# A fused attention and two-layer MoE kernel: routing of the second layer with a tightened span, three rounds for three more experts, and rows turned later

## The chip, the cores and the metric

The kernel runs on one core of a Trainium2 chip. The metric is the device time of one execution in microseconds (us); lower is better. The traces are taken by the hardware profiler on one execution.

## What is computed

The reference chains three parts. Attention: 4 batches, 8 heads, 768 positions, head size 64, a causal window of 128 and 4 sink positions. A first mixture of experts (MoE): each of the 3072 tokens (512 features) goes to the expert with its largest logit. A second MoE, the part that the change touches: every expert takes exactly 384 tokens, given out greedily over the sorted logits.

```python
def _moe2_ref(x, w_gate, w1, w2):
    N, D, E, F = (3072, 512, 8, 1024)
    cap = N // E
    logits = x @ w_gate
    order = np.argsort(-logits.flatten())
    for idx in order:                 # largest logit first
        tok, e = (int(idx) // E, int(idx) % E)
        if assigned[tok] >= 0 or counts[e] >= cap:
            continue
        assigned[tok] = e
        counts[e] += 1
    for e in range(E):
        h = np.maximum(x[assigned == e] @ w1[e], 0.0)
        out[assigned == e] = h @ w2[e]
```

## The kernel before, in words

The change is in the second MoE, which starts at about 519 us. Two things run interleaved there, in one program order that the Python code writes out.

**The expert FFN** (`Ffn.run`, from L823). The experts are worked off one after the other, 384 tokens each, in 8 chunks s of 128 hidden features. A chunk is 12 matmuls into ph (L1036: four parts d of the 512 features, three products each of a high and a low part, in place of one float32 product), then ScalarE's relu hh (L1046) and VectorE's remainder hl (L1047), and 9 matmuls into y0 to y2 (L950, helper mm3) for an earlier chunk. Weights are split into high and low parts ahead of use: w1h, w2h on ScalarE (L917, L897), w1l on VectorE or POOL (L922), w2l on POOL (L901).

Between groups of matmuls of a chunk, `side(q)` (L995) is called for q = 0 to 3: after half of the ph matmuls, after all of them, after the first y group, at the end. It splits a weight, turns rows, and calls `tick` (L942), which calls the router's `pop`, asks for weights (`poll_w`) and for the next gather (`poll_x`, L874). `src.pop()` offers the router three more places in a chunk.

**Turning rows.** An expert's rows come by three indirect DMAs (parts a) into xg, issued by POOL (`xget`, L1890). They must be transposed: `xprep` (L789) does it for one of four feature parts d: three transposes on TensorE into the PSUM bank tr (L796), ScalarE's high part xh (L797), VectorE's low part xl (L798). There is one bank tr, so a turning waits until both have read the one before. The tuple xp says at which (chunk of the expert, q) the next expert's parts are turned: (6,0), (6,2), (7,0), (7,2).

**The router** (`Route.steps`, L1914) finds for the next expert in order the logit bound above which exactly 384 free tokens lie. One round `it` compares all best logits with 64 bounds (`compare`, L1675, on VectorE), counts by 13 small matmuls (L1693, helper `count`), compares the counts with 384 (gs, gg), spreads the result by one matmul (L1976), takes maxima (J8), and sets the next, 62 times finer bounds (b0, b1, lop, lo). POOL keeps a 1x1 copy of b0 (L1957). Experts 0 to 2 in this order have three rounds each (L1940: `last`), experts 3 to 6 have four; the eighth takes what is left. After the rounds the chosen tokens A are taken out of L, and the span for the next expert's first round is set from the last bound and lb[k+1], a lower bound that the preparation before had found (L2012 to L2016).

**Compaction** (`compact`, L1899, `compact_steps`, L1482) turns A into a list of 384 row numbers idx: a prefix matmul (L1498), one-hot compares on VectorE, 26 matmuls (L1523). Then the gather may be issued.

**The order.** `Route.pop` (L1829) is offered a place some seven times per chunk, and issues a step of the compaction and one of the rounds, each only if the planner's TensorE clock has come to the time the step asked for, and if its VectorE clock is at most half a microsecond ahead of TensorE's (SLACK). These clocks are the planner's estimates; they set only the order of the program. `force_x` (L1874) issues compaction steps without asking when rows are to be turned and no list is there.

The end of expert k's second layer is copied out by `yout` (L2051) and scattered by indirect DMAs on POOL (L2055).

Of the kernel before, what the change touches and what calls it, by code (L numbers as in the profile page):

```python
# [779 lines left out]
class Ffn:  # L780
# [42 lines left out]
    def run(self, js, w1, w2, src, yout, hook=None, xp=((6, 0), (6, 2), (7, 0), (7, 2)), LEAD=3, LAG=2, pre=None, onx=None, more=(), mark=lambda s, n: None):  # L823
# [108 lines left out]
        def prep(j, d, tag="tr"):  # L932
            if j not in xgs:
                src.force_x(j)
                clk.pe = max(clk.pe, clk.dve)
                wantx.remove(j)
                xgs[j] = src.xget(j)
            if d == 0 and onx is not None:
                onx(j, xgs[j])
            self.xprep(j, src.width(j), xgs[j], d, tag)  # L940

        def tick():  # L942
# [3 lines left out]
            poll_x()  # L946
# [44 lines left out]
        for s in range(last + 1):  # L991
# [3 lines left out]
            def side(q):  # L995
# [9 lines left out]
                if jx + 1 < len(js) and s < total:  # L1005
                    for d in range(4):
                        if xp[d] == (f, q):
                            prep(js[jx + 1], d)
                if not ticked:
# [89 lines left out]
class Src:  # L1099
# [15 lines left out]
    wait = 0  # L1115

# [352 lines left out]
SLACK = 0.5  # L1469
SLACK1 = 1.6  # L1470
# [80 lines left out]
class Route(Src):  # L1551
# [4 lines left out]
    def __init__(self, nc, g, pool, xs):  # L1556
# [4 lines left out]
        self.em3 = {}  # L1561
        self.at = [0.0, 0.0]
# [30 lines left out]
         self.half, self.nrow, self.hi, self.J2, self.nv) = (self.sc[:, i:i + 1] for i in range(17))  # L1593
# [59 lines left out]
    def sizes(self, V, pd):  # L1653
# [3 lines left out]
        V.tensor_scalar(self.nrow, self.nbig, 2.0, None, op0=OP.mult)  # L1657

# [170 lines left out]
    def pop(self):  # L1829
        clk = self.g.clk  # L1830
        for i, f in ((1, self.pop_comp), (0, self.pop_main)):
            if clk.pe >= self.at[i] and clk.dve < clk.pe + (SLACK if 1 in self.idx else SLACK1):
# [57 lines left out]
    def xget(self, k):  # L1890
        xg = self.x[k] if k in self.x else self.xp.tile([128, 3, DM], F32, name="xg2", bufs=2)
        for a in range(3):
            self.nc.gpsimd.indirect_dma_start(out=xg[:, a, :], out_offset=None, in_=self.xs,
                                              in_offset=bass.IndirectOffsetOnAxis(ap=self.idx[k][0][:, a:a + 1], axis=0))
        em = self.em3[k] = self.p.tile([1, 1], I32, name="em3", bufs=E)
        self.nc.gpsimd.tensor_copy(em, self.e[k])
        return xg

# [15 lines left out]
    def steps(self):  # L1914
# [16 lines left out]
        for k in range(E):  # L1931
# [4 lines left out]
            if k < E - 1:  # L1936
# [3 lines left out]
                last = NIT - 1 if k == 0 or k > FEW else NIT - 2  # L1940
                for it in range(first, last + 1):
# [11 lines left out]
                    else:  # L1953
                        self.compare(V, slice(0, 2), slice(0, HR), inv)
                        V.tensor_scalar(b0, d, -1.5, lo0 if it == 0 else lo, op0=OP.mult, op1=OP.add)
# [71 lines left out]
            else:  # L2027
# [4 lines left out]
                V.tensor_copy(em, t0[0:1])  # L2032
                nc.tensor.matmul(pc, g.ones, OH, start=True, stop=True, skip_group_check=True)
                nc.scalar.activation(junk, pc, AF.Copy, accum_out=chk[:, 0, k:k + 1])
                self.e[k] = em
                self.comp.append(self.compact(k, A, rs, pre))
# [244 lines left out]
```

## Time and profile before

| | |
|---|---|
| median of 3 runs | 852.79 us (852.39 to 853.32) |
| profiled execution | 853.57 us, span 851.8 us |
| mean granted TensorE clock | 0.992 |
| TensorE busy | 813.5 us, 96% of the span |
| VectorE, ScalarE, POOL busy | 608.7, 384.9, 348.0 us |
| longest chain to the end | PE 78%, DVE 11%, ACT 4% |

In the profile PE is TensorE, PEld its weight load, DVE VectorE, ACT ScalarE, POOL GpSimd, SP the engine that issues most DMAs. A line such as `ph L1036` names the tile and the line of the kernel; all of the router's VectorE instructions have L145, since a helper issues them, and are told apart by their tiles. A duration is that of one instruction as the profiler gives it; matmuls are pipelined, so the time that one holds TensorE's queue is read from its start to the next one's start. In timelines, instructions of one kind in a row are merged (x13), and `[1.13 <-DMA ...]` says how long the engine was idle before and what ended it.

### The profile page before, as it was taken

How to read it: one execution, taken by the hardware profiler on the slowest of the kernel's cores; microseconds unless marked ns; L12 is line 12 of the kernel's file. 1: busy time of each engine (PE TensorE's matmuls, PEld its weight loads, DVE VectorE, ACT ScalarE, POOL GpSimd, SP SyncE). 2: the span in 40 equal slices, each digit the busy share in tenths (PEclk: the TensorE clock that was granted, in tenths of full speed). 3: DMA queues.
4: the chain of work that ended last, by engine and by line, in shares of the span. 5: the costliest groups of instructions: out<-in, count | busy, mean ns of one | idle time of the engine just before them, and what ended most of it. 6: DMA issues, size and time to landing. Idle time of an engine off the chain costs nothing.

```text
span 851.8 us, 15197 instructions
## 1 busy us (share of the span) xinstructions
PE 813.5 (96%) x5001; PEld 651.6 (76%) x5006; DVE 608.7 (71%) x1763; ACT 384.9 (45%) x1091; POOL 348.0 (41%) x574
## 2 busy tenths in 40 slices
PE   8889999998999999999999988999999999999997
PEld 4666666667888888888888746778888888889996
DVE  7888787877579696978878268868688787753320
ACT  6667777764342433344342313334334343434442
POOL 5455967582331101020000004436465656465662
PEclk9999999999999999999999998999999999999999
DMA  7434555666534544444436507334444345345401
GB/s 222 159 107 150 151 144 143 176 217 215 120 84 166 161 136 149 149 148 126 124 104 223 192 14 235 126 110 149 145 155 146 129 151 154 126 161 174 147 39 42
DMA packets 70655, 122.85 MB, mean 144 GB/s; under 512 B 9890, under 2 KB 24102, under 8 KB 70440
## 3 DMA queue, kind: packets, MB, share of 16 engines
q1 hardware_dynamic: 63848, 102.36, 38.0%
q0 software_dynamic: 6720, 19.43, 7.1%
q8 instruction: 42, 0.69, 0.4%
q14 instruction: 45, 0.37, 0.2%
HBM read 102.06 MB, written 19.71 MB: 143 GB/s over the span
## 4 chain that ended last, share of the span: by engine, by line
PE 78%; DVE 11%; ACT 4%; issue 3%; DMA 1%; POOL 1%; DVEq 0%; POOLq 0%; ACTq 0%
PE y L950 29%; PE ph L1036 28%; PE sp L323 4%; PE po L395 3%; ACT P L352 3%; PE tr L796 2%; PE rt L1693 2%; PE pt L360 2%; PE px L431 1%; PE rc L1523 1%; DMA xg<-xs,idx 1%; DVE mx L342 1%; DVE sc L145 1%; PE sp L409 1%; DVE sp L340 1%
## 5 line engine op out<-in xcount | busy, mean ns | idle before, releaser
L1046 ACT ACTIVATE hh<-ph 128x384 fp32r<-128x384 f32 (+1 forms) x112 | 60.2, 538 | 268.2 <-PE ph L1036 267.6
L1036 PE MATMUL ph<-xh,w1h 128*128 128x384 f32 (+1 forms) x448 | 166.9, 372 | 0.8 <-DVE hl L1047 0.8
L1036 PE MATMUL ph<-xh,w1l 128*128 128x384 f32 (+1 forms) x448 | 161.1, 360 | 1.2 <-DVE w1l L922 1.2
L1036 PE MATMUL ph<-xl,w1h 128*128 128x384 f32 (+1 forms) x448 | 160.4, 360 | 0.0
L950 PE MATMUL y<-w2h,hh 128*128 128x512 f32 x384 | 153.6, 400 | 0.0
L950 PE MATMUL y<-w2h,hl 128*128 128x512 f32 x384 | 150.9, 393 | 0.0
L950 PE MATMUL y<-w2l,hh 128*128 128x512 f32 x384 | 150.5, 392 | 0.0
L1047 DVE SCALAR_TENSOR_TENSOR hl<-ph,hh 128x384 fp32r<-128x384 f32 (+1 forms) x112 | 68.4, 612 | 98.6 <-ACT hh L1046 98.1
L1201 POOL DMA_INDIRECT xg<-xd,ent x26 | 28.0, 1078 | 195.0 <-DMA ent<-idtab 189.8
L1225 DVE SCALAR_TENSOR_TENSOR junk<-yr,wgb 128x512 f32<-128x512 f32 x160 | 103.1, 685 | 0.0
L901 POOL TENSOR_TENSOR w2l<-w2r,w2h 128x512 fp32r<-128x512 f32 x60 | 79.2, 1326 | 46.1 <-ACT w2h L897 22.2
L1036 PEld LDWEIGHTS ph<-xh,w1h 128*128 128x128 f32 x448 | 85.0, 190 | 12.6 <-issue 1.9
L1036 PEld LDWEIGHTS ph<-xh,w1l 128*128 128x128 f32 x448 | 84.3, 188 | 11.1 <-DVE w1l L922 1.6
L352 ACT ACTIVATE P<-sp,mx 128x132 f32<-128x132 f32 x192 | 69.3, 369 | 51.5 <-DVE mx L342 18.7
L1036 PEld LDWEIGHTS ph<-xl,w1h 128*128 128x128 f32 x448 | 84.0, 188 | 7.7
L950 PEld LDWEIGHTS y<-w2h,hl 128*128 128x128 f32 x384 | 72.0, 188 | 15.6
L950 PEld LDWEIGHTS y<-w2h,hh 128*128 128x128 f32 x384 | 72.6, 189 | 11.5 <-issue 0.2
L950 PEld LDWEIGHTS y<-w2l,hh 128*128 128x128 f32 x384 | 72.2, 188 | 11.7
L323 PE MATMUL sp<-kr,qs 64*128 64x260 f32 (+1 forms) x384 | 58.6, 402 | 13.7 <-ACT P L352 12.5
L917 ACT ACTIVATE w1h<-w1r 128x512 fp32r<-128x512 f32 x108 | 67.3, 624 | 2.1 <-DVE lp L449 2.1
L897 ACT ACTIVATE w2h<-w2r 128x512 fp32r<-128x512 f32 x108 | 67.5, 625 | 0.0
L922 DVE TENSOR_TENSOR w1l<-w1r,w1h 128x512 fp32r<-128x512 f32 x78 | 63.8, 818 | 2.4 <-ACT w1h L917 2.4
(394 smaller groups left out, 1401.9 us busy)
## 6 DMA issues: line engine op xcount, KB each, us to landing
w1r<-in_w_dram SPq DMA_DIRECT2D x29, 1024.0 KB, 5.8
w2r<-in_w_dram SPq DMA_DIRECT2D x29, 1024.0 KB, 5.9
vr<-in_v_dram SPq DMA_DIRECT2D x16, 384.0 KB, 4.9
xd<-xb SPq DMA_DIRECT2D x16, 384.0 KB, 3.5
xs<-yr SPq DMA_DIRECT2D x24, 256.0 KB, 6.1
kr<-in_kT_dram SPq DMA_DIRECT2D x15, 396.0 KB, 3.8
qr<-in_qT_dram SPq DMA_DIRECT2D x15, 384.0 KB, 4.3
wgb<-in_wg2T_dram SPq DMA_DIRECT2D x1, 2048.0 KB, 8.4
```

Of the source, the lines that this page charges most:

```text
L323: nc.tensor.matmul(sp[:, hd, c0:260], qs[o:o + 64, 128 * i:128 * i + 128], kr[o:o + 64, k0:k0 + 260 - c0], start=True, stop=True)
L352: nc.scalar.activation(z.P[:, n % 2, hd, :], s.sp[:, hd, 128:260], AF.Exp, bias=s.mx[:, hd:hd + 1], accum_out=z.sm[:, n % 2, hd:hd + 1])
L897: nc.scalar.activation(ch[1][c][0], r[q // 2][:, q % 2, :] if isinstance(r, list) else r[:, q, :], AF.Copy)
L901: eng.tensor_tensor(lo, r[q // 2][:, q % 2, :] if isinstance(r, list) else r[:, q, :], h.bitcast(F32), op=OP.subtract)
L917: nc.scalar.activation(h, v, AF.Copy)
L922: eng.tensor_tensor(lo, v, h.bitcast(F32), op=OP.subtract)
L950: nc.tensor.matmul(o, l, r, start=(first and i == 0), stop=(end and i == 2))
L1036: nc.tensor.matmul(ph, wp[:, c, :], xp_[:, c, 0:NTK], start=(d == 0 and i == 0), stop=(d == 3 and i == len(cut[d]) - 1))
L1046: nc.scalar.activation(hh, ph, AF.Relu)
L1047: nc.vector.scalar_tensor_tensor(hl, ph, 0.0, hh.bitcast(F32), op0=OP.max, op1=OP.subtract)
L1201: self.nc.gpsimd.indirect_dma_start(out=self.xg[j][:, a, :], out_offset=None, in_=self.G.xd[0:k, :], in_offset=bass.IndirectOffsetOnAxis(a ...
L1225: nc.vector.scalar_tensor_tensor(junk, yr[:, 0:DM], 1.0, wgb[:, e, :], op0=OP.mult, op1=OP.mult, accum_out=lg[:, e:e + 1])
```

## The change

Five edits, all in the second MoE.

1. In the second round of experts 1 to 4 (k < E - 3, k > 0), four VectorE operations on 128x1 values raise lb[k+1], the lower end of the next expert's first span: to the bound of the second-best expert in this round, but at least LEAST (0.04 of the largest logit) under the present bound. One more operation in the preparation (`sizes`) computes that distance.
2. `last` makes it three rounds for experts 3 to 5; experts 0 (its rounds counted 1 to 3) and 6 keep theirs.
3. `quiet`: from half a chunk ahead of the first turning to the last one, `pop` issues no compaction step, once expert 1's list is there. Rounds go on.
4. `xp2`: the rows of experts 1 and 2 are turned at (6,2), (7,0), (7,1), (7,2).
5. The three gathers of experts 3 to 7 are issued one per tick (`more`), those of experts 0 to 2 at once as before; and the last expert's check matmul is issued later, after its compaction is queued.

```diff
--- before.py
+++ after.py
@@ -820,7 +820,7 @@
         for _ in range(k):
             self.nc.tensor.matmul(p, self.g.wz[:, 0:128], self.g.wz, start=True, stop=True)
 
-    def run(self, js, w1, w2, src, yout, hook=None, xp=((6, 0), (6, 2), (7, 0), (7, 2)), LEAD=3, LAG=2, pre=None, onx=None, more=(), mark=lambda s, n: None):
+    def run(self, js, w1, w2, src, yout, hook=None, xp=((6, 0), (6, 2), (7, 0), (7, 2)), LEAD=3, LAG=2, pre=None, onx=None, more=(), mark=lambda s, n: None, xp2=None):
 
 
         nc, wk, ps, clk = self.nc, self.wk, self.ps, self.g.clk
@@ -935,6 +935,7 @@
                 clk.pe = max(clk.pe, clk.dve)
                 wantx.remove(j)
                 xgs[j] = src.xget(j)
+            src.more()
             if d == 0 and onx is not None:
                 onx(j, xgs[j])
             self.xprep(j, src.width(j), xgs[j], d, tag)
@@ -943,7 +944,10 @@
             if hook is not None:
                 hook()
             poll_w(2)
-            poll_x()
+            if src.parts:
+                src.more(1)
+            else:
+                poll_x()
 
         def mm3(o, pairs, w, first, end):
             for i, (l, r) in enumerate(pairs):
@@ -1003,9 +1007,11 @@
                 else:
                     split(s, q)
                 if jx + 1 < len(js) and s < total:
+                    at = xp2 if xp2 and jx < 2 else xp
                     for d in range(4):
-                        if xp[d] == (f, q):
+                        if at[d] == (f, q):
                             prep(js[jx + 1], d)
+                    src.quiet = at[0] <= divmod(4 * f + q + 2, 4) and (f, q) < at[3]
                 if not ticked:
                     tick()
 
@@ -1113,6 +1119,10 @@
 
     force_x = xids = force_e
     wait = 0
+    parts = ()
+
+    def more(self, n=3):
+        pass
 
     def ereg2(self, j):
         return self.ereg(j)
@@ -1467,6 +1477,7 @@
 JC, NIT, FEW, IDLE = 64, 4, 2, (3, 2, 1)
 WARM, WARM1, WA = 9, 3, (7, 4, 3, 2)
 SLACK = 0.5
+LEAST = 0.04
 SLACK1 = 1.6
 XO = 9
 X0 = 2.0
@@ -1559,6 +1570,7 @@
         self.gen = self.steps()
         self.comp = []
         self.em3 = {}
+        self.quiet = False
         self.at = [0.0, 0.0]
         p = pool
         self.L = p.tile([128, NR, E], F32, name="L")
@@ -1590,7 +1602,7 @@
         self.chk = p.tile([128, 3, E], F32, name="chk")
         self.want = p.tile([128, 3, E], F32, name="chw")
         (self.lo0, self.lo, self.lop, self.b0, self.b1, self.J, self.esum, self.eidx, self.bad, self.t0, self.nbig, self.span,
-         self.half, self.nrow, self.hi, self.J2, self.nv) = (self.sc[:, i:i + 1] for i in range(17))
+         self.half, self.nrow, self.hi, self.J2, self.nv, self.next, self.least, self.none) = (self.sc[:, i:i + 1] for i in range(20))
 
     def setup(self):
 
@@ -1655,6 +1667,7 @@
         V.tensor_scalar(self.nbig, self.half, 1e-20, -16.0, op0=OP.max, op1=OP.mult)
         V.tensor_scalar(self.half, self.nbig, 0.5, None, op0=OP.mult)
         V.tensor_scalar(self.nrow, self.nbig, 2.0, None, op0=OP.mult)
+        V.tensor_scalar(self.least, self.nbig, -LEAST / 16.0, None, op0=OP.mult)
 
     def widths(self, V, dd, o, span):
         V.tensor_scalar(dd[:, 0, o:NIT], self.pw[:, 0:NIT - o], span, 1e-30, op0=OP.mult, op1=OP.max)
@@ -1829,6 +1842,8 @@
     def pop(self):
         clk = self.g.clk
         for i, f in ((1, self.pop_comp), (0, self.pop_main)):
+            if i == 1 and self.quiet and 1 in self.idx:
+                continue
             if clk.pe >= self.at[i] and clk.dve < clk.pe + (SLACK if 1 in self.idx else SLACK1):
                 f()
 
@@ -1889,12 +1904,21 @@
 
     def xget(self, k):
         xg = self.x[k] if k in self.x else self.xp.tile([128, 3, DM], F32, name="xg2", bufs=2)
-        for a in range(3):
+
+        def part(a):
             self.nc.gpsimd.indirect_dma_start(out=xg[:, a, :], out_offset=None, in_=self.xs,
                                               in_offset=bass.IndirectOffsetOnAxis(ap=self.idx[k][0][:, a:a + 1], axis=0))
-        em = self.em3[k] = self.p.tile([1, 1], I32, name="em3", bufs=E)
-        self.nc.gpsimd.tensor_copy(em, self.e[k])
+            if a == 2:
+                em = self.em3[k] = self.p.tile([1, 1], I32, name="em3", bufs=E)
+                self.nc.gpsimd.tensor_copy(em, self.e[k])
+        self.parts = [lambda a=a: part(a) for a in range(3)]
+        self.more(1 if k > FEW else 3)
         return xg
+
+    def more(self, n=3):
+        for f in self.parts[0:n]:
+            f()
+        del self.parts[0:n]
 
     def compact(self, k, A, rs, pre):
         def check(cnt):
@@ -1937,7 +1961,7 @@
                 dd = self.dd1 if k == 0 else dn
                 lo0 = self.lb[:, k:k + 1]
                 first = 1 if k == 0 else 0
-                last = NIT - 1 if k == 0 or k > FEW else NIT - 2
+                last = NIT - 1 if k in (0, E - 2) else NIT - 2
                 for it in range(first, last + 1):
                     d, inv = dd[:, 0, it:it + 1], dd[:, 1, it:it + 1]
                     if k == 0:
@@ -1952,6 +1976,12 @@
                             V.tensor_scalar(b0, d, -1.5, lo, op0=OP.mult, op1=OP.add)
                     else:
                         self.compare(V, slice(0, 2), slice(0, HR), inv)
+                        if it == first + 1 and k < E - 3:
+                            low = self.lb[:, k + 1:k + 2]
+                            V.tensor_scalar(self.none, J8[:, 1:2], 0.5, nbig, op0=OP.is_lt, op1=OP.mult)
+                            V.tensor_scalar(self.next, J8[:, 1:2], dd[:, 0, first:it], b0, op0=OP.mult, op1=OP.add)
+                            V.scalar_tensor_tensor(self.next, lo, self.least, self.next, op0=OP.subtract, op1=OP.min)
+                            V.scalar_tensor_tensor(low, self.next, self.none, low, op0=OP.add, op1=OP.max)
                         V.tensor_scalar(b0, d, -1.5, lo0 if it == 0 else lo, op0=OP.mult, op1=OP.add)
                         if it > 0:
                             nc.gpsimd.tensor_copy(self.hold[:, it - 1:it], b0[0:1])
@@ -2030,10 +2060,11 @@
                 V.tensor_scalar(t0, esum, -1.0, float(E * (E - 1) // 2), op0=OP.mult, op1=OP.add)
                 V.tensor_scalar(t0, t0, 0.0, float(E - 1), op0=OP.max, op1=OP.min)
                 V.tensor_copy(em, t0[0:1])
+                self.e[k] = em
+                self.comp.append(self.compact(k, A, rs, pre))
+                yield max(clk.dve, clk.pe) + 1.0
                 nc.tensor.matmul(pc, g.ones, OH, start=True, stop=True, skip_group_check=True)
                 nc.scalar.activation(junk, pc, AF.Copy, accum_out=chk[:, 0, k:k + 1])
-                self.e[k] = em
-                self.comp.append(self.compact(k, A, rs, pre))
                 yield 0.0
 
 
@@ -2060,7 +2091,7 @@
             if k < E - 1 and a == 2:
                 nc.gpsimd.drain()
 
-        f.run(list(range(E)), w1, w2, rt, yout, hook=rt.pop, xp=((6, 0), (6, 2), (7, 0), (7, 2)))
+        f.run(list(range(E)), w1, w2, rt, yout, hook=rt.pop, xp=((6, 0), (6, 2), (7, 0), (7, 2)), xp2=((6, 2), (7, 0), (7, 1), (7, 2)))
         bi = g.cp.tile([1, 1], I32, name="bi")
         nc.vector.tensor_copy(bi, rt.bad[0:1])
     return nc.values_load(bi, min_val=0, max_val=1)
```

## Rows read from the trace of the kernel before

**Rows 1.** Busy time of each engine by stage: PE, PEld, DVE, ACT, POOL, PEclk, DMA

```profile
524.00:680.00 156.00, 149.78 (x979) 129.22 (x979) 121.20 (x329) 59.81 (x138) 86.16 (x90) 1.00 0.43 146
680.00:842.00 162.00, 161.32 (x930) 143.37 (x930) 85.78 (x188) 67.85 (x146) 91.81 (x92) 1.00 0.38 126
```

**Rows 2.** PE's waits from 520 to 852 us: total, times, longest

```profile
PE tr L796 <- DMA xg<-xs,idx: 3.2, 4, 1.1
PE rt L1693 <- DVE cmp L145: 1.1, 1, 1.1
...
PE rc L2033 <- DVE OH L145: 0.7, 1, 0.7
```

**Rows 3.** PE's timeline around one search round's matmuls: start, duration

```profile
671.67 0.18 PE L1976 MATMUL rt<-gg,ones 128*128 128x8 bf16 x1
671.71 0.42 PE L1036 MATMUL ph<-xh,w1h 128*128 128x384 f32 x1
...
682.42 0.95 PE L1693 MATMUL rt<-OH,cmp 128*128 128x16 bf16 x13
683.23 0.42 PE L1036 MATMUL ph<-xh,w1h 128*128 128x384 f32 x1
683.48 0.34 PE L1036 MATMUL ph<-xh,w1l 128*128 128x384 f32 x1
```

**Rows 4.** Timeline of DVE and POOL ahead of the late compare

```profile
672.11 3.18 DVE L145 SCALAR_TENSOR_TENSOR sc<-J8m,dd,sc 128x1 f32<-128x1 f32 x2
...
673.86 1.28 POOL L901 TENSOR_TENSOR w2l<-w2r,w2h 128x512 fp32r<-128x512 f32 x1
```

**Rows 5.** Timeline of DVE and PE at the second layer's start

```profile
522.92 0.46 DVE L145 TENSOR_SCALAR sc<-dd,sc 128x1 f32<-128x1 f32 x2
...
529.74 0.45 PE L1036 MATMUL ph<-xh,w1h 128*128 128x384 f32 x1 [0.79 <-DVE hl L1047]
```

**Rows 6.** Instructions of the tile J8m: ns min/median/max, first and last start

```profile
L145 DVE SCALAR_TENSOR_TENSOR sc<-J8m,dd,sc x41: 206/220/3048, 504.2 to 728.4; 128x1 f32<-128x1 f32 x41
```

**Rows 7.** POOL's wait at the 1x1 copy, 520 to 852 us: total, times, longest

```profile
POOL hold L1957 <- DVE sc L145: 31.1, 12, 5.4
```

**Rows 8.** PE's timeline where expert 1's rows are turned

```profile
552.63 0.27 PE L796 MATMUL tr<-cst,xg 128*128 128x128 f32 x1
...
555.34 0.42 PE L1036 MATMUL ph<-xh,w1h 128*128 128x384 f32 x1
...
557.16 0.49 PE L796 MATMUL tr<-cst,xg 128*128 128x128 f32 x3
557.40 0.47 PE L950 MATMUL y<-w2h,hh 128*128 128x512 f32 x1
```

**Rows 9.** PE's timeline where expert 2's rows are turned

```profile
598.16 0.27 PE L796 MATMUL tr<-cst,xg 128*128 128x128 f32 x1
...
600.04 0.42 PE L1036 MATMUL ph<-xh,w1h 128*128 128x384 f32 x1
```

**Rows 10.** Timeline of all engines around expert 2's turning at (7,0)

```profile
604.78 0.49 PE L796 MATMUL tr<-cst,xg 128*128 128x128 f32 x3
...
605.84 0.56 DVE L798 TENSOR_TENSOR xl<-tr,xh 128x384 fp32r<-128x384 f32 x1 [0.41 <-ACT xh L797]
...
606.18 0.39 PE L950 MATMUL y<-w2h,hh 128*128 128x512 f32 x1
...
606.87 0.49 PE L796 MATMUL tr<-cst,xg 128*128 128x128 f32 x3
```

**Rows 11.** Timeline of all engines around expert 1's turning at (7,0)

```profile
560.98 0.49 PE L796 MATMUL tr<-cst,xg 128*128 128x128 f32 x3
...
562.74 0.55 DVE L798 TENSOR_TENSOR xl<-tr,xh 128x384 fp32r<-128x384 f32 x1
```

**Rows 12.** Timeline of PE and POOL: expert 2's compaction and last gather part

```profile
589.81 0.56 PE L1523 MATMUL rc<-ft,ohb 128*128 128x12 bf16 x7
...
596.24 1.11 POOL L1893 DMA_INDIRECT xg<-xs,idx  x1 [0.30 <-PE y L950]
```

## The prediction

> **What bounds the kernel now.** I read the page's busy shares first, then the busy time by stage. From 524 us, where the second layer's experts begin, TensorE is busy 149.78 of 156 us and then 161.32 of 162 us, at a granted clock of 1.00, the upper of its two levels (2.4 GHz) [rows 1]. VectorE, which does most of the routing arithmetic, has 121 of 156 us and then 86 of 162. So the second layer lasts as long as TensorE's work plus the few stops of its in-order queue. Every instruction taken from that queue shortens the end one for one; work taken from another engine does so only where TensorE was stopped by it. The list of TensorE's waits from 520 us on gives the stops: 3.2 us for gathered rows, 1.1 us for one compare, 0.7 us for the last expert's one-hot [rows 2]; a few smaller ones, most before 545 us, are not touched by the change.
>
> The sum is made against the profiled execution, 853.57 us (span 851.8). It lies 0.78 us above the median of the three timed runs (852.79) and just above the highest of them (853.32), so I take the difference off the median at the end. A measurement of this kernel can tell about 0.2% from no change, 1.7 us: below 851.1 is faster, above 854.5 slower.
>
> **Three rounds fewer.** Experts 3, 4 and 5 each lose their fourth search round. A round puts on TensorE 13 count matmuls, which hold the queue from 682.42 to 683.23, 0.81 us, after which the next matmul's pitch is 0.25 us instead of 0.18 (0.07), and one small matmul, 671.67 to 671.71, 0.04 us, with a like refill [rows 3]: 1.0 us. All of it stands between FFN matmuls that follow without a gap, so nothing hides it and nothing else takes its place. Three rounds: **-3.0 us**. Their VectorE work and three 1x1 copies on POOL's queue go as well, worth nothing by themselves, as TensorE is not waiting for them.
>
> **The compare that came late.** The one 1.1 us stop of a count has a visible cause. VectorE's two small products of that round took 3.18 us, from 672.11 to 675.29, and they ended as POOL finished the w2l of 673.86 to 675.14 [rows 4]: POOL had worked off w1l and w2l back to back behind three gather issues in a row. The change issues gathers of experts 3 to 7 one part per tick, so POOL's backlog is shorter, but the other rounds still meet POOL somewhere. Bounds: 0 and -1.1 us. I take half, **-0.5 us**.
>
> **The last one-hot.** The last expert's check matmul (L2033) is put after at least 1 us of planned work. Its 0.7 us stop [rows 2] goes, and what is queued behind it is FFN work whose inputs are ready: **-0.7 us**. If the next group of VectorE work stood in the way instead, it would be 0.
>
> **The added VectorE operations.** Experts 1 to 4 get four 128x1 operations each in their second round, behind the compare and ahead of the bound values. Two such took 0.46 us [rows 5], so four take 0.9 us. For experts 2 to 4 I cost them at nothing against TensorE (beyond the turning below): VectorE has over 30 us free in the first of the two stretches. Without that cover it would be 0.9 us each. For expert 1 they fall at 522.9, just before the first FFN matmuls, ahead of the low parts of the first tile's rows, and this same VectorE queue is what stops TensorE at 529.74 for 0.79 us [rows 5]. So here they lie on the path: **+0.9 us**, between 0, if a slack that I don't see takes them up, and 1.1, with the single extra setup operation near 486 us, which else hides behind the first layer's tail.
>
> Two of the four read two SBUF tensors. The nearest operation of that kind, the 128x1 product with the round's maximum, takes 220 ns in the median but up to 3048 [rows 6], and the long ones end with a POOL operation as in [rows 4]. Against that, POOL is in order and mostly stands waiting at its 1x1 copy of the very value computed behind the new operations, 31.1 us in 12 waits [rows 7], so it is idle when they run; I take the unblocked price. The Trainium skill, page "SBUF — State Buffer", section "Who interferes with whom", says that a VectorE instruction with two SBUF inputs and a GpSimd instruction that reads SBUF exclude each other for the whole instruction. By that rule alone each new pair could wait out a POOL operation, which is the first rival; rows 4 agree with it.
>
> **The rows of experts 1 and 2.** Now the first of four turnings stands at (6,0) (chunk 6, after the second group of matmuls) and waits for the gather. For expert 1 it holds TensorE from 552.63 to 555.34, where three transposes take 0.24 (557.16 to 557.40): 2.47 us lost [rows 8]. For expert 2, 598.16 to 600.04: 1.64 us lost [rows 9]. Together 4.1 us. The change puts the turnings at (6,2), (7,0), (7,1), (7,2). From (6,0) to (6,2) are 1.82 us, 1.75 without the refill (555.34 to 557.16, [rows 8]). That covers expert 2's wait but leaves 0.7 us of expert 1's.
>
> What is late next is the single PSUM bank that all turnings share: a turning may start only when ScalarE and VectorE have read the one before. With both engines free, VectorE's read starts 1.06 us after the transposes and takes 0.56, so the bank is free 1.62 us after a turning starts, while TensorE comes to the next place, (7,1), after 1.40 (604.78 to 606.18) [rows 10]. With the semaphore's delay that is a stop of 0.25 us. The turning at (7,1) then frees the bank 1.62 us after its own start, while TensorE needs only its 0.24, the first second-layer group (0.69) and a refill (0.08) to reach (7,2): a stop of 0.6. So 0.85 us at the least per expert. For expert 1 the trace shows VectorE full in this very place: a round's compare and bounds put the read off to 562.74, 2.31 us after the transposes to its end [rows 11]. With the 0.9 us of new operations ahead of it this becomes 3.2, against 1.40: a stop of 1.8, plus 0.6 at (7,2), so 2.4. I take 2.4 for expert 1 and 0.85 for expert 2, whose (7,0) shows a free VectorE [rows 10]. New cost 0.7 + 2.4 + 0.85 = 3.95, old 4.1: **-0.15 us**. The bounds: 0.85 each and 0.3 of gather, -2.1; 2.4 each, 0.7, and 0.9 for a gather of expert 2 that its added operations put off, +2.3.
>
> **Costed at nothing.** Holding back compaction while rows are turned delays gathers of experts 3 to 7, which landed before they were asked for: all of TensorE's gather waits belong to experts 1 and 2 (2.47 and 1.64 lost hold the whole 3.2 of [rows 2]), and one round fewer makes them earlier. The DMAs issued stay the same in number and size. The second half of each expert's weights waits for a copy that now comes two ticks later; it is due some four chunks after the first half, so SP's queue holds nothing up. If this cover failed, TensorE would wait for weights, and no row of before shows such a wait.
>
> **Sum:** -3.0 - 0.5 - 0.7 + 0.9 - 0.15 = -3.45 us: 850.1 for the profiled execution, **849.3** on the median.
>
> **The rivals.**
> *New operations caught behind POOL.* If POOL is at work when the two-input operations come, each pair waits for one operation of 1.28 us (as the w2l in [rows 4]), once at the start and once ahead of the turning at (7,0) of expert 1: 2.6 us less gain, 851.9, no measurable change. For it: 3048 ns [rows 6]; against: POOL's standing wait [rows 7]. The section of "SBUF — State Buffer" in the Trainium skill named above is the rule behind this rival.
>
> *The round misses the turning.* The planner issues routing work only where its account of VectorE is not over half a microsecond ahead of TensorE's; three close turnings fill that account. If expert 2's second round is thereby put behind the turnings, both experts pay 0.85 and expert 1 little more than 0.3 of gather: -2.1 there, the full -1.1 for the compare, in all -6.0: 846.8.
>
> *Compaction of expert 2 caught by the hold.* This is the one that makes it slower. If that compaction has not ended when the hold begins, shortly before TensorE reaches 598.16, nothing issues it until the turning at (6,2) forces it, and TensorE stands still from the compaction's matmuls to the landing: 589.81 to 600.04, 10 us now, with the last gather part issued at 596.24 [rows 9, 12], of which some 9 would be new: 858. It decides from a delay of 8 us of the row at 589.81; I count 0.9 of added operations and perhaps one lost place of some 3.5 us. So unlikely.
>
> *The change does not do what it says.* If three rounds left a group other than 384 tokens, the kernel's own counts would send it into its general path, hundreds of us more. The tightened first span makes the last step finer, not coarser, so I give it 1 in 100.
>
> **The numbers.** Forecast 0.48, missed turning 0.26, caught behind POOL 0.17, hold 0.08, general path 0.01. Faster: all of the missed turning and most of the forecast, 0.68. Same: caught behind POOL and the forecast's upper edge, 0.22. Slower: hold, general path and the edge of the turnings' upper bound, 0.10. The range runs from 846.0 (missed turning, with the added operations hidden) to 852.4 (caught behind POOL, a little over); the hold and the general path are left out.
>
> **What would show it.** 19 search rounds instead of 22 for experts 1 to 6, and TensorE's busy time from 524 us down by about 3 us; no stop of L2033; a gather wait of at most 0.7 us at expert 1 and none at expert 2; in its place, stops of the transposes for VectorE's reading of the bank at (7,1) and (7,2) of experts 1 and 2, 3 us in all; the first hl stop still there and all later rows 0.9 us later against the first gather. If the transposes stop for VectorE much less or more than 3 us, that term was mis-sized; if TensorE stops for gathers by several us at expert 2, the hold caught it and the forecast is wrong in sign.

## The result and the profile after

The kernel became slower: 863.57 us (median of 6 runs, 859.95 to 865.60) against 853.06 (852.39 to 853.91), ratio 1.0106 with a 95% interval of 1.0086 to 1.0126. I had forecast 849.3 and a range up to 852.4: the sign was wrong. The profiled execution after took 863.25 us (span 861.5), 9.7 more than the one before.

The busy time by stage of the kernel after answers to [rows 1]; columns are stretch, its length, busy time of PE, PEld, DVE, ACT, POOL with instruction counts, granted clock, DMA share, GB/s.

```profile
524.00:680.00 156.00, 148.66 (x951) 127.41 (x951) 121.91 (x326) 60.20 (x142) 84.97 (x89) 1.00 0.42 139
680.00:842.00 162.00, 153.92 (x867) 136.92 (x866) 79.33 (x175) 66.43 (x140) 89.98 (x89) 0.98 0.39 132
```

TensorE stands still 7.34 + 8.08 = 15.4 us there; before it was 6.22 + 0.68 = 6.9. That is +8.5, in stretches of equal time; the kernel after has more of its work left behind them. The three rounds are gone as meant (in the whole trace the count line falls from 325 records to 286, 3 x 13), -3.0 by my sum. PE's waits from 520 us on, of the kernel after (total, times, longest), answer to [rows 2]:

```profile
PE tr L796 <- DVE xl L798: 5.7, 6, 1.6
PE rt L1706 <- DVE cmp L145: 4.3, 1, 4.3
PE rc L1509 <- DVE A L145: 2.4, 2, 2.0
...
PE tr L796 <- DMA xg<-xs,idx: 0.6, 1, 0.6
```

The gather waits fell from 3.2 to 0.6 and the last one-hot's stop is gone, as forecast. In their place stand a compare of 4.33 us and an A of 2.04 us, in the timeline of PE of the kernel after:

```profile
686.34 0.95 PE L1706 MATMUL rt<-OH,cmp 128*128 128x16 bf16 x13 [4.33 <-DVE cmp L145]
...
725.23 0.16 PE L1509 MATMUL rc<-rs,tri 128*128 128x1 bf16 x1 [2.04 <-DVE A L145]
```

Behind the first of them TensorE's clock falls (busy time in stretches of 2 us, same columns as above):

```profile
684.00:686.00 2.00, 0.00 (x0) 0.00 (x0) 1.82 (x7) 0.00 (x0) 0.00 (x0) 1.00 0.67 246
686.00:688.00 2.00, 1.66 (x17) 1.67 (x18) 1.73 (x7) 0.41 (x3) 0.00 (x0) 0.77 0.00 0
688.00:690.00 2.00, 2.00 (x9) 1.90 (x8) 0.29 (x1) 0.55 (x2) 1.28 (x1) 0.50 0.03 8
690.00:692.00 2.00, 2.00 (x11) 1.81 (x10) 0.61 (x2) 1.07 (x3) 0.00 (x0) 0.87 0.00 0
...
708.00:710.00 2.00, 2.00 (x27) 1.72 (x25) 0.46 (x4) 0.78 (x2) 1.84 (x3) 1.00 0.12 38
710.00:712.00 2.00, 2.00 (x18) 1.96 (x18) 0.94 (x3) 1.11 (x2) 1.54 (x5) 0.75 0.38 152
712.00:714.00 2.00, 2.00 (x9) 1.70 (x8) 0.87 (x6) 0.00 (x0) 0.84 (x1) 0.50 0.58 238
714.00:716.00 2.00, 2.00 (x10) 1.78 (x10) 1.59 (x3) 1.03 (x3) 0.34 (x1) 0.90 0.01 4
```

0.50 is the lower of its two levels, 1.2 GHz. Lost, by my estimate: 2 x (0.23 + 0.50 + 0.13) = 1.7 us. A like dip stands from 710 to 716 us, another 1.7, with no stop ahead of it. The ledger of the two whole profiled executions: TensorE's idle time is 861.5 - 814.9 = 46.6 us against 851.8 - 813.5 = 38.3, +8.3; its busy time rose by 1.4, in which the rounds are -3.0 and the clock +3.4, and 1.0 is not accounted for. Together that is the 9.7 us.

Why was the compare late? The timeline of VectorE of the kernel after, through the selection, the step that makes A of the last round's bound (`oc` is the product that starts it, `pre` the scan behind A, `sc<-J8m` the product with the round's maximum just ahead of it):

```profile
674.73 0.22 DVE L145 SCALAR_TENSOR_TENSOR sc<-J8m,dd,sc 128x1 f32<-128x1 f32 x1
...
675.12 0.27 DVE L145 TENSOR_TENSOR oc<-OH,ce 128x224 bf16<-128x224 bf16 x1
...
676.14 5.67 DVE L145 TENSOR_TENSOR_SCAN pre<-ones,A 128x28 f32<-128x28 bf16 x1
...
720.06 4.40 DVE L145 TENSOR_TENSOR oc<-OH,ce 128x224 bf16<-128x224 bf16 x1
...
725.21 0.22 DVE L145 TENSOR_TENSOR_SCAN pre<-ones,A 128x28 f32<-128x28 bf16 x1
```

and POOL's beside it:

```profile
674.00 1.25 POOL L1909 DMA_INDIRECT xg<-xs,idx  x1 [0.16 <-issue]
675.25 0.18 POOL L1987 COPY hold<-sc 1x1 f32<-1x1 f32 x1
675.60 0.97 POOL L1909 DMA_INDIRECT xg<-xs,idx  x1 [0.16 <-issue]
...
676.71 2.52 POOL L901 TENSOR_TENSOR w2l<-w2r,w2h 128x512 fp32r<-128x512 f32 x2
679.20 1.29 POOL L922 TENSOR_TENSOR w1l<-w1r,w1h 128x512 fp32r<-128x512 f32 x1
680.46 1.28 POOL L901 TENSOR_TENSOR w2l<-w2r,w2h 128x512 fp32r<-128x512 f32 x1
...
719.45 0.96 POOL L1909 DMA_INDIRECT xg<-xs,idx  x1 [0.16 <-issue]
720.56 1.30 POOL L922 TENSOR_TENSOR w1l<-w1r,w1h 128x512 fp32r<-128x512 f32 x1
721.83 2.50 POOL L901 TENSOR_TENSOR w2l<-w2r,w2h 128x512 fp32r<-128x512 f32 x2
```

A scan that takes 0.22 us alone (725.21) takes 5.67 and ends at 681.81, as POOL's four splits in a row end (681.74); a product of 0.27 us takes 4.40 and ends at 724.46, as three splits end (724.33). Both read two SBUF tensors. So the mechanism of [rows 4] has come back longer, at the selection, because gathers of one expert and the selection of the next now fall together: both long operations began while the last gather was being issued. Worked out from the timelines, the time from the end of an expert's last gather issue to the next expert's oc:

| kernel | expert 2 | expert 3 | expert 4 | expert 5 |
|---|---|---|---|---|
| before | 13.5 | 12.7 | 15.7 | 16.5 us |
| after | 14.8 | 7.2 | -1.5 | -0.4 us |

From one oc to the next it is 36 to 41 us before, about what an expert's FFN takes. With three rounds it is 31 to 34 (oc at 610.55, 641.19, 675.12): the search runs ahead of the FFN until it meets the gathers, which stay tied to the FFN.

### The profile page after: what moved, and what is told of

The parts are those of the page before. It is cut to its first block, busy times and chain, and to the rows that moved or that the text cites. A ratio compares the mean times of both kernels' runs of the same rounds, so it can differ in the third digit from the quotient of the medians.

```text
span 861.5 us, 15107 instructions
## 1 busy us (share of the span) xinstructions
PE 814.9 (95%) x4959; PEld 652.2 (76%) x4964; DVE 604.0 (70%) x1753; ACT 385.5 (45%) x1091; POOL 347.0 (40%) x571
## 4 chain that ended last, share of the span: by engine, by line
PE 74%; DVE 15%; ACT 5%; issue 4%; POOL 1%; DMA 0%; POOLq 0%; DVEq 0%; ACTq 0%
PE ph L1042 27%; PE y L954 26%; PE sp L323 4%; PE po L395 3%; ACT P L352 3%; PE tr L796 2%; PE rt L1706 2%; PE pt L360 2%; PE px L431 2%; PE rc L1534 1%; DVE mx L342 1%; DVE sc L145 1%; DVE pre L145 1%; PE sp L409 1%; DVE cmp L145 1%
## 5 line engine op out<-in xcount | busy, mean ns | idle before, releaser
L954 PEld LDWEIGHTS y<-w2h,hl 128*128 128x128 f32 x384 | 72.0, 188 | 15.6
L922 DVE TENSOR_TENSOR w1l<-w1r,w1h 128x512 fp32r<-128x512 f32 x78 | 59.9, 768 | 2.4 <-ACT w1h L917 2.4
```

Source lines behind the costliest of these rows:

```text
L922: eng.tensor_tensor(lo, v, h.bitcast(F32), op=OP.subtract)
L954: nc.tensor.matmul(o, l, r, start=(first and i == 0), stop=(end and i == 2))
```

## The experiments

All against the kernel before, run in the same jobs:

| run | median us | ratio [95%] |
|---|---|---|
| a1 gathers at once | 864.20 | 1.0116 [1.0087, 1.0145] |
| a2 no hold | 864.99 | 1.0123 [1.0091, 1.0156] |
| a3 four rounds | 859.94 | 1.0066 [1.0043, 1.0089] |
| a4 rows early | 858.72 | 1.0047 [1.0023, 1.0071] |
| b1 rounds only | 864.94 | 1.0128 [1.0109, 1.0146] |
| f0 rounds undone too | 856.46 | 1.0033 [1.0023, 1.0043] |
| b2 four rounds, no hold | 860.16 | 1.0073 [1.0056, 1.0089] |
| c1 hold behind scan | 872.60 | 1.0199 [1.0157, 1.0241] |
| c3 the same, rows early | 865.41 | 1.0136 [1.0108, 1.0165] |
| e2 one more copy | 862.99 | 1.0110 [1.0086, 1.0134] |
| g1 rounds only, pause | 849.63 | 0.9956 [0.9940, 0.9973] |
| g2 whole change, pause | 885.32 | 1.0366 [1.0342, 1.0390] |
| h1 POOL at selection | 859.37 | 1.0064 [1.0042, 1.0087] |
| h2 POOL in pause | 850.34 | 0.9957 [0.9937, 0.9977] |
| h3 pause, no hold | 878.70 | 1.0293 [1.0246, 1.0340] |
| h4 pause, rows later | 878.36 | 1.0296 [1.0240, 1.0352] |
| i1 rows later in phase | 849.99 | 0.9936 [0.9916, 0.9956] |
| i2 whole change in phase | 851.53 | 0.9961 [0.9942, 0.9981] |

**Which part of the change?** Each of the first four undoes one part.

```diff
a1 -        self.more(1 if k > FEW else 3)
   +        self.more(3)
a2 -                    src.quiet = at[0] <= divmod(4 * f + q + 2, 4) and (f, q) < at[3]
   +                    src.quiet = False
a3 -                last = NIT - 1 if k in (0, E - 2) else NIT - 2
   +                last = NIT - 1 if k == 0 or k > FEW else NIT - 2
a4 -        f.run(..., xp2=((6, 2), (7, 0), (7, 1), (7, 2)))
   +        f.run(...)
```

> The changed kernel, but the three gathers of experts 3 to 7 are issued at once again. Theory A (one part per tick mixes gathers and low-part subtractions on POOL, so that POOL falls behind and then works off four subtractions back to back, and a two-input VectorE operation behind that waits it out): the 5.67 and 4.40 us VectorE operations near 676 and 720 us shrink to about 3 us or less, TensorE's stops of 4.3 and 2.0 us go, and the time falls by 6 us or more, to 857 or below. Theory B (the three fewer rounds move the selection of the next expert onto the gather of the last one, however that is issued): the time stays within 2 us of 863.6. Theory C (holding back compaction moves gathers onto selections): also within 2 us.

> The changed kernel without the hold of compaction while rows are turned. Theory C (the hold moves gathers onto selections): the long VectorE operations go and the time falls by 6 us or more. Theory A (gathers one part per tick) and theory B (three fewer rounds): still 860 or more, since gathers and rounds are as in the changed kernel; a shift of the places where POOL and VectorE meet may move it by 3 us either way.

> The changed kernel with the fourth round of experts 3 to 5 put back. Theory B (fewer rounds bring selection and gather together): the long VectorE operations go, and although TensorE has 3 us more work, the time falls by 3 us or more, to 860 or below. Theory A (gathers one part per tick): long VectorE operations stay and the time rises by the 3 us of TensorE's work, to about 866. Theory C: about 866 as well.

> The changed kernel with the rows of experts 1 and 2 turned at the places of before. My sum of the turnings said that the move is worth 0.15 us: the stops for VectorE's reading of the bank at (7,1) and (7,2), 2.6 us in the changed profile for experts 1 and 2, go, and gather waits of about 3 us come back, so the time stays within 1 us of 863.6. Theories A, B and C all expect the 4.3 and 2.0 us stops near 686 and 725 us to stay, unless the shift of about a chunk's part moves them.

Neither the gathers by parts nor the hold matters here: a1 and a2 are as slow as the change, with long operations of 5.82 and 4.63 us, so theories A and C fail. With four rounds (a3), as theory B says, no VectorE operation over 2.2 us is left after 600 us, but two gather waits of expert 3 come, of 1.27 and 2.62 us. For a4 I had expected no effect; it took 4.9 us off: the 4.40 us operation is gone, and in place of the 5.67 us scan an oc takes 4.43 us at 674. Moving the rows moves the meetings.

**The rounds by themselves.** b1 is the kernel before with only the rounds, the added operations that they need, and the later last check; f0 takes the rounds out of b1 again; b2 is a3 without the hold.

```diff
b1 = after with a1, a2 and a4
f0 = b1 with a3
b2 = a3 with a2
```

> The kernel before with only the shorter search of experts 3 to 5 (and the added VectorE operations that make it safe, and the later last check): gathers in one go, no hold of compaction, rows at the old places. Meeting theory (one round fewer moves the selection of the next expert onto POOL's backlog behind a gather; a round also carries a 1x1 copy on POOL that breaks this backlog up): VectorE shows operations of over 3.5 us in the selection after 620 us, TensorE stops behind them, and the time is 854 to 862, no faster than before. Rival (the rounds themselves are a gain, and the other parts of the change brought the loss): 850 to 852, no VectorE operation over 3.2 us.

> The run with the rounds alone (864.9), with its three rounds undone as well: what is left of the change is the VectorE operations added in the second round of experts 1 to 4, the setup operation and the later last check. Meeting theory (the loss comes from the missing rounds): within 1.5 us of the kernel before, 0.9 for the added operations less 0.7 for the last check. Rival (the added operations put VectorE's work late at every expert): 858 or more.

> The changed kernel with four rounds for experts 3 to 5 as before, and compaction not held while rows are turned. The run with four rounds and the hold took 859.9, with gather stops of 1.27 and 2.62 us at expert 3. Hold theory: these two stops go, 855 to 857. Rival (expert 3's gather is late because its parts are issued one by one, or for the added operations): the stops stay, 859 to 861.

b1 is as slow as the whole change, 3 us above the range that I gave it; f0 is 8.5 us faster than b1 (8.1 by the ratios): taking out three rounds of 1 us each costs that much. In b1 the product with J8m, just ahead of expert 5's oc, takes 4.70 us, and later a turning waits 4.17 us for xl behind compaction and compares on VectorE:

```profile
671.53 4.70 DVE L145 SCALAR_TENSOR_TENSOR sc<-J8m,dd,sc 128x1 f32<-128x1 f32 x1
...
692.38 0.90 PE L796 MATMUL tr<-cst,xg 128*128 128x128 f32 x3 [4.17 <-DVE xl L798]
```

From the last gather to the next oc b1 has 9.8, 8.2, 4.3 and 10.3 us; in the 4.3 lies the wait of that product, which began while the last gather was being issued. f0 lies 2.4 us above before, more than the 1.5 that I allowed: this is what the added operations and the later last check cost by themselves. In b2 the two gather waits stay (0.64 and 2.52 us): the hold did not make them.

**Can POOL be made to wait?** In the program's order POOL's 1x1 copies (H) stand between its splits. One line per kernel (G a gather issue, or three that follow each other; EM the copy of the expert's number; 1 and 2 a split of w1 and of w2), from the scatters at about 662 us to the next ones:

```
before  2 G EM H 1 2 H 2 1 H 2 2 1 2 2 1 2
after   H 2 G 1 G H G EM 2 2 1 2 2 H 1 2 2 1 H 2
b1      G EM H 2 1 2 2 1 2 2 1 H 2 G EM H 2 1 H 2
g1      2 1 2 H 2 G EM 1 H 2 2 1 2 2 1 2
```

A copy waits for VectorE's b0, and so breaks POOL's backlog into pieces. c1 moves the last round's copy behind the scan, c3 does so with the rows early, e2 keeps all copies and adds that one.

```diff
c1 -                        if it > 0:
   +                        if 0 < it < last:
                                 nc.gpsimd.tensor_copy(self.hold[:, it - 1:it], b0[0:1])
   ...
                     pre = prefix(V, g, p, A, "")
   +                if k > 0:
   +                    nc.gpsimd.tensor_copy(self.hold[:, last - 1:last], pre[0:1, 0:1])
c3 = c1 with a4
e2 = after with
   +                if k > 0:
   +                    nc.gpsimd.tensor_copy(self.hold[:, NIT - 1:NIT], pre[0:1, 0:1])
```

> The changed kernel, with POOL's 1x1 copy of the last round taken from behind the last bounds to behind the scan of the selection, so that the POOL operations that follow it in the queue start only when the selection's two-input operations are over. Same work, one operation moved. Meeting theory: the 5.67 us scan and the 4.40 us product fall under 2.5 us, TensorE's stops of 4.3 and 2.0 us and the fall of its clock go: 852 to 857. Rival (the three rounds give VectorE's selection too little room, whatever POOL does, or the POOL work now late stops TensorE on w1l or w2l): 860 or more, with stops released by POOL.

> As the run before it, with the rows of experts 1 and 2 turned at the old places. Rows early took 4.9 us off the changed kernel. If that gain was its own (the bank stops of 3.2 us against gather stops), it stays: 2 to 5 us below the run before. If it came from moving the meetings of selection and POOL, it is gone: within 1 us of the run before, the gather stops of some 2 to 4 us in place of the bank stops.

> The changed kernel, with one more 1x1 copy on POOL behind the scan of each selection of experts 1 to 6 and all its other copies kept: POOL then stands still until the scan is over. If POOL's unbroken train of splits alone makes the loss: the scan takes under 2 us, the stops of 4.3 and 2.0 us go, 853 to 858. If the shifted phase costs through VectorE's own backlog too (turnings, compares and compaction one behind the other): the scan is short but other stops of 2 us and more stand elsewhere, 860 to 866.

c1 missed by far: without the last round's copy the backlog fell on an earlier product with J8m (4.44 us at 639.75). That agrees with what the copy is taken to do. c1's longer stops are VectorE's (compares 6.1 us, the bank 6.5), none is POOL's, which the rival had expected. c3 lies 7.2 us below c1 (5.4 by the ratios), more than either of its two cases said: the rows early gain again, but by no fixed amount, and i1 below shows that they gain nothing in phase. e2 removed the long scan, and nothing was gained. VectorE's timeline in e2:

```profile
674.39 1.90 DVE L145 TENSOR_TENSOR oc<-OH,ce 128x224 bf16<-128x224 bf16 x1
...
677.04 0.22 DVE L145 TENSOR_TENSOR_SCAN pre<-ones,A 128x28 f32<-128x28 bf16 x1
...
677.89 1.09 DVE L145 SCALAR_TENSOR_TENSOR L<-ce,sc,L 128x224 f32<-128x224 bf16 x1
678.91 1.28 DVE L145 SCALAR_TENSOR_TENSOR tm<-A,sc,tm 128x28 f32<-128x28 bf16 x1
...
680.41 1.00 DVE L145 TENSOR_TENSOR sc<-sc 128x1 f32<-128x1 f32 x1
```

The waiting went to four other two-input operations. Against their times in the kernel after (0.27, 0.43, 0.23, 0.14 us) they took 4.2 us longer, where the scan had taken 5.45 longer; the compare's stop is still 3.01 us. POOL's splits were not fewer; they met other two-input operations.

**Put the phase back.** g1 is b1 with a pause of the planner where the fourth round had been; no instruction is added. g2 is the whole change with it.

```diff
+                if FEW < k < E - 2:
+                    yield clk.pe + 8.0
                 ce = p.tile([128, E], BF, name="ce")
```

> The run with the rounds alone, and in the place of each missing fourth round of experts 3 to 5 a pause of the planner of 8 us that issues no instruction, so that gathers, rounds and selections fall into the same part of every expert, as they do before. Meeting theory: no VectorE operation over 3.3 us after 640 us, TensorE's stops of more than 1.5 us go, the three rounds are gained: 850 to 853. Rival (fewer rounds or the narrower span cost by themselves, wherever they stand): 860 or more.

> The changed kernel whole, with the same pause of 8 us in place of each missing fourth round. Meeting theory: the 5.67 and 4.40 us operations and the stops of 4.3 and 2.0 us go with the fall of the clock; the bank stops of experts 1 and 2 (3.1 us) stay: 851 to 855. Rival: the selection meets the gathers again, 860 or more.

g1 takes 849.63 us, 15 us less than b1 and faster than both kernels. From the last gather to the next oc it has 17.0, 14.9, 16.7 and 15.6 us. Its busy time by stage:

```profile
524.00:680.00 156.00, 150.25 (x969) 130.49 (x968) 116.55 (x321) 62.01 (x142) 86.80 (x91) 1.00 0.45 147
680.00:842.00 162.00, 162.00 (x924) 143.81 (x923) 77.92 (x185) 67.60 (x145) 91.55 (x93) 1.00 0.38 126
```

No stop at all from 680 to 842 us. Against f0, which has the three rounds and no pause and is otherwise the same, g1 is 6.8 us faster. In the profiled executions it is 6.0 of span: 3.6 less busy time of TensorE, and 2.4 less idle time, as a compare's stop of 1.07 us and the last check's of 1.14 are gone.

g2 missed badly: with its later rows and the full pause expert 3's oc comes at 618.71, in g1 at 613.63, and gathers were late at experts 3, 4 and 5 (2.53 us at 643.05, 4.24 at 697.41, 4.37 at 750.76). h3 (g2 without the hold) and h4 (g1 with later rows) take it apart; i1 and i2 are h4 and g2 with a shorter pause for expert 3, after which expert 3's oc stands at 613.71 in i1 and POOL's order shows gathers and selections in the place that they have in g1, or one split from it.

```diff
h3 = g2 with a2
h4 = g1 with xp2=((6, 2), (7, 0), (7, 1), (7, 2))
i1 = h4 and i2 = g2, with
-                    yield clk.pe + 8.0
+                    yield clk.pe + (4.0 if k == FEW + 1 else 8.0)
```

> The changed kernel with the pause (885.3), and compaction not held while rows are turned; gathers one part a tick and later rows are kept. Hold theory: the gather stops of 4 to 5 us at each of experts 3 to 5 came from the hold, and go: 850 to 856. Rival (they came from the gathers' parts being issued one a tick, or from the later rows): 865 or more, with the stops still there.

> The run with the rounds alone and the pause (849.6), with the rows of experts 1 and 2 turned at the later places. By the stops read (3.8 us of gathers and bank at experts 1 and 2 against 3.1 in the changed kernel): 849, within 1.5 us. If the later rows put VectorE's work off for the experts behind them: 852 or more, with new stops after 600 us.

> The run with later rows and the pause (878.4), with the pause of expert 3 cut from 8 to 4 us: the planner then issues gathers and selections of experts 3 to 5 in the same place of every expert as in the run of 849.6 us, where with the full pause they came some two splits later. Phase theory: the gather stops of experts 3 to 5 (2.6, 1.5 and 1.0 us and two more at each) go: 848 to 852. Rival (later rows put expert 3's gather off whatever the phase): 860 or more.

> The whole change with the same pauses (4 us at expert 3, 8 at 4 and 5): rows later, gathers a part a tick, compaction held while rows are turned. If the hold costs nothing once compaction has ended ahead of it: within 2 us of the run without the hold and the split gathers that goes with it, 848 to 853. If the hold still catches compaction: gather stops of 2 to 5 us at experts 3 to 5, 858 to 875.

The hold theory of h3 and my 849 for h4 missed. h3 and h4 are alike: gathers by parts cost nothing, later rows out of phase cost 29 us, the hold on top 6.6 (h3 to g2). In phase the later rows cost nothing: i1 differs from h4 by one number of the plan, 4 us for 8 at expert 3, and is 28.4 us faster. The whole change in phase takes 851.53 us: 0.4% faster than before, where without the pause it is 1.1% slower. Of the three gather waits left in i2 (2.0 us; i1 has none) the two behind 600 us, in PE's timeline:

```profile
681.00 0.33 PE L796 MATMUL tr<-cst,xg 128*128 128x128 f32 x1 [0.66 <-DMA xg<-xs,idx]
...
721.55 0.33 PE L796 MATMUL tr<-cst,xg 128*128 128x128 f32 x1 [0.59 <-DMA xg<-xs,idx]
```

**POOL's work by itself.** h1 and h2 add to g1 the same POOL work for experts 3 to 5, behind or ahead of the pause; VectorE and TensorE have as many instructions as in g1.

```diff
+                    nc.gpsimd.tensor_copy(self.hold[:, NIT - 1:NIT], J8[0:1, 0:1])
+                    for _ in range(4):
+                        nc.gpsimd.tensor_tensor(self.extra, self.g.wz, self.g.wz, op=OP.mult)
```

> The run with the rounds alone and the pause (849.6), with a 1x1 copy and four 128x512 products of two SBUF tensors added on POOL behind the pause of experts 3, 4 and 5, so that they run while VectorE does the selection. Nothing is added on VectorE or TensorE. Lock theory: in each of the three selections VectorE's two-input operations take longer by about the length of the four POOL operations in all, TensorE stops behind them, some 3 to 8 us an expert: 856 to 872. Rival (POOL's work matters only by making the low parts of the weights late): the same time as the run with the four products ahead of the pause.

> The same copy and four POOL products, ahead of the pause instead of behind it, where VectorE has next to no operation of two SBUF inputs. Lock theory: within 2.5 us of the run without them (849.6), and VectorE's selection is not stretched. Rival (POOL's lateness): the same time as the run with the four products behind the pause.

The place alone is worth 9.0 us. (h1's profiled execution is its fastest, 856.49 us, 5.1 above h2's, so the traces account for 5.1 of the 9.0.) h1, POOL and then VectorE:

```profile
614.50 4.41 POOL L2019 TENSOR_TENSOR extra<-wz 128x512 bf16<-128x512 bf16 x4
618.88 1.28 POOL L901 TENSOR_TENSOR w2l<-w2r,w2h 128x512 fp32r<-128x512 f32 x1
```

```profile
613.24 1.26 DVE L145 TENSOR_TENSOR oc<-OH,ce 128x224 bf16<-128x224 bf16 x1
...
615.63 1.10 DVE L145 TENSOR_TENSOR_SCAN pre<-ones,A 128x28 f32<-128x28 bf16 x1
...
616.90 1.12 DVE L145 SCALAR_TENSOR_TENSOR L<-ce,sc,L 128x224 f32<-128x224 bf16 x1
617.94 1.02 DVE L145 SCALAR_TENSOR_TENSOR tm<-A,sc,tm 128x28 f32<-128x28 bf16 x1
...
619.18 1.00 DVE L145 TENSOR_TENSOR sc<-sc 128x1 f32<-128x1 f32 x1
...
620.32 0.46 DVE L145 TENSOR_TENSOR OH<-L,S__77 128x224 bf16<-128x224 f32 x1
```

The same two operations in h2, from VectorE's timeline, and then a stop of TensorE in h1:

```profile
614.07 1.32 DVE L145 TENSOR_TENSOR oc<-OH,ce 128x224 bf16<-128x224 bf16 x1
...
616.63 0.22 DVE L145 TENSOR_TENSOR_SCAN pre<-ones,A 128x28 f32<-128x28 bf16 x1
```

```profile
631.50 0.17 PE L2007 MATMUL rt<-gg,ones 128*128 128x8 bf16 x1 [3.31 <-DVE gg L145]
```

From oc to OH it is 7.1 us in h1, 4.1 in h2 (614.07 to 618.16). TensorE in h1 stops for gg 3.31 us here and 1.23 at each of the two experts behind; h2 has no such stop there. So POOL's work costs through VectorE, and not by being late itself.

## Why the prediction was wrong

The steps about TensorE's own queue held. **Three rounds, -3.0:** the work went as priced (3.6 us less busy time in g1 than in f0). **Rows of experts 1 and 2:** new stops 0.56 for the gather and 1.63 + 0.48 + 0.48 for the bank, 3.15 in all against 3.95 forecast; the stops before were 3.2 by the same list (4.1 as I counted them, from start to start); i1 beside g1 shows no difference in time (849.99 and 849.63), as forecast (-0.15). **Added operations at the start, +0.9:** the hl stop moved from 529.74 to 530.53, 0.8. **Last one-hot, -0.7:** gone after, but in f0 the same matmul stops 1.14 us for ScalarE, so the gain hangs on the place.

**The step that failed** is the one that let the schedule stand: that the VectorE work and the three 1x1 copies that go with a round are "worth nothing by themselves", and that earlier gathers are harmless. The time that a round takes in the plan was what kept the search in step with the FFN and POOL's backlog away from the selection. Without it the selection met the backlog: stops of 4.3 and 2.0 us, the clock behind the first, turnings that wait for VectorE at later experts (5.7 us of bank stops in all, where 2.6 are those of experts 1 and 2). b1 against f0 shows the price, 8.5 us more instead of 3.0 less; g1, and i1 beside h4, show that the phase makes it, not the missing rounds. The missing copies do not make it by themselves either: g1 lacks them too.

**The late compare, -0.5,** was wrong in sign with its reason: with gathers at once (a1) the time is the same and the long operation is no shorter, and the stop became 4.3 us.

The rival that saw the mechanism, *new operations caught behind POOL*, was put at the added operations and priced at one POOL operation, 1.28 us each; it came at the selection and held VectorE for three and four operations. My reason against it, that POOL "mostly stands waiting" at its copy, was a misreading of [rows 7]: 31.1 us in 332 us of time are less than a tenth. The Trainium skill, page "SBUF — State Buffer", section "Who interferes with whom", has the rule that such a pair excludes each other for the whole instruction; h1 and h2 agree (a scan of 1.10 and 0.22 us); the scan of 5.67 us, which waited for four POOL operations one after the other, goes beyond it. *Compaction caught by the hold* did not come at expert 2 in the change as made, but it is real at later experts: 6.6 us in g2 over h3. *The round misses the turning* did not come.

With the phase kept, the whole change gives 3.4 us (851.53 against 854.91 in its job), where my sum said 3.45. Part of that nearness is luck: f0 shows the added operations and the last check together at +2.4, where I had +0.2 (new there are bank stops of 0.95 and 0.96 us at experts 1 and 2 and the last check's 1.14), and g1 against f0 shows the rounds in phase at -6.8, where I had -3.0, or -3.5 with the compare.

Not settled: how the 10.5 us divide between VectorE held off by POOL and VectorE's own queue at turnings. They feed each other, and in e2 taking the one away only moved it.

## What to carry to other kernels

Where two loops of nearly one period share engines, the work of a step also sets the phase: take the step out, and something else meets. Compare the periods after the change, and where they differ, keep the phase by a pause in the plan before judging the saving. A list of an engine's instructions in program order, a line per period, shows such a drift without any time in it.

## What was not expected of the hardware

A VectorE operation with two SBUF inputs can be kept out for a whole row of POOL operations (5.67 us instead of 0.22, four splits), while in h1 others got in after one POOL operation each (1.10 us). What decides between the two no run here shows. Most of the long ones (the scan, the two oc of 4.40 and 4.43 us, the products with J8m of 4.70 and 4.44) began while POOL was issuing a gather; but so did the oc at 675.12, which took 0.27 us.

And the clock can fall with no stop right ahead of it: after 39 small matmuls in 3.2 us (26 of compaction from 707.67 on, 13 of a count at 710.04, with three large ones between) the kernel after ran at 0.50 from 712 to 714 us, though TensorE had been busy without a break from 706 us on. The matmuls by themselves do not settle it: the same 26 and 13 left the clock at 1.00 in the kernel before (626.99 and 629.36) and were followed by 0.50 in i1 (630.88 and 633.25, the clock from 636 to 638 us).
